# QKV projections as 64-row products in both row halves, with spread-out score maxima that add in PSUM

## The chip, the cores and the metric

The kernel runs on one core of a Trainium2 chip. The core has a matrix engine (TensorE, PE in the profile; its weight loads are listed apart as PEld), three engines for elementwise work (VectorE is DVE, ScalarE is ACT, GpSimd is POOL) and a queue that starts DMA transfers (SyncE, SP). Products land in PSUM, of which this kernel uses eight banks of 128 x 512 fp32. The metric is the time on the device in microseconds (us), the median over runs.

## The reference, cut to what matters

A transformer block on 2048 tokens of width 640, in fp32: layer norm, attention with 32 heads of 20, a residual, layer norm, a SwiGLU feed-forward of width 1728, a residual.

```python
B, S, D, H = 1, 2048, 640, 32            # F = 1728
def _A_ref(x, wqkv, wo):
    qkv = (x @ wqkv).reshape(B, S, 3, H, Dh).transpose(2, 0, 3, 1, 4)
    q, k, v = qkv[0], qkv[1], qkv[2]
    scores = einsum("bhqd,bhkd->bhqk", q, k) * (Dh ** -0.5)
    p = softmax(scores, axis=-1)
    o = einsum("bhqk,bhkd->bhqd", p, v)
    return o.transpose(0, 2, 1, 3).reshape(B, S, D) @ wo
h  = x + _A_ref(layernorm(x), wqkv, wo)
h2 = h + (silu(layernorm(h) @ w_gate) * (layernorm(h) @ w_up)) @ w_down
```

Here the projections `x @ wqkv` matter, and the row maxima of the scores that the softmax subtracts.

## The kernel before

**Precision.** fp32 operands are split into a high and a low part of a narrower type (`split`, L84): ScalarE rounds the high part, VectorE or GpSimd subtracts. A product is then three: high by high, low by high, high by low. With a depth of 640 = 5 x 128 rows, each output block takes 15 products that add up in one PSUM bank.

**Stages.** Layer norm, QKV projections and a part of the score maxima come first (to 367.6 us), then attention, the output projection and the feed-forward. The order of the instructions of every engine is the order in which the program issues them; no planner moves them. Only the first stage differs between the two kernels.

**The projection stage.** The tokens come in four chunks `c` of 512. A chunk has 18 slots (counted over the chunks in `slot[0]`): ten query or key blocks of 128 rows of the transposed result (`query_key`, 15 products of 128 rows and 512 columns, L447) and eight value halves (`value`, 15 products of 320 columns, L523), keys first. In the first chunk the first two blocks are made together by `first_blocks` (L471), and the slot after them is empty. When a block is done, `keep` copies it out of PSUM, splits it and stores it to memory (L486 to L513; the splits wait in `halved` for the next slot); for values, L531 copies. In the course of a chunk the next one is normalised (`norm`, L121, L122, L95 and L401 on VectorE, one or two steps behind each slot) and turned by transposes (`flip`, L417).

**The maxima.** The softmax of a later stage needs, for each query, the greatest score. A unit is a group of four heads (eight groups) and a query chunk. Two heads lie in rows 0 to 59 of a stacked tile and two in rows 64 to 123; so a product of 60 rows uses one row half of TensorE, and the `b` loop issues one for each half. `pair` picks the first or second head of a half, `t` the 128 queries, `kc` the key chunk. Some of the maxima are found during the projections, to fill VectorE's and ScalarE's time: all of unit 0 (`max_pair`, L171, one reduction over both 512-column results at L180), and key chunks 0 and 1 of several other units (`max_halves`, L182). For the latter the stored keys also hold, for half a chunk, the differences of two halves k1 - k2, so that the greater of two scores is q.k2 + relu(q.(k1 - k2)): a 512-column product gives q.k2 and q.(k1 - k2) side by side, ScalarE takes the positive part of the second into SBUF (L193), and VectorE adds and takes the maximum in one custom instruction for each row half (L195).

**What sets the order.** `urgent` (unit 0) and `early` (the rest) are lists of such jobs with a condition, mostly that the staged keys and queries were loaded at least two slots ago. `visit(n)` runs up to n of them; it is called once inside every block and value half and once after it, so that TensorE gets a cluster of two or three pairs of 60-row products. Staged keys and queries are loaded back from memory by `load_items` into five places, four of them shared with the raw weights (`raw`) and one apart (`fifth`); `stored_at` says from which slot on they are in memory.

**PSUM in this stage.** `ps_wide` has three places of two banks (maxima, and the first blocks), `ps_one` two places of one bank (projections and transposes).

Of the kernel before, what the change touches and what calls it, by code (L numbers as in the profile page):

```python
# [9 lines left out]
F32 = mybir.dt.float32  # L10
# [34 lines left out]
def tile_block(ctx: ExitStack, tc: tile.TileContext, x, wqkv, wo, wg, wu, wd, out):  # L45
# [125 lines left out]
    def max_pair(mx, q, k, pair, t, kc, k0):  # L171

        ps = ps_wide()
        for b in range(2):
            rows = slice(b * ROW, b * ROW + NPART)
            nc.tensor.matmul(
                ps[:, b, :], q[rows, pair, t * P : (t + 1) * P], k[rows, pair, k0 : k0 + CH],
                start=True, stop=True,
            )
        nc.vector.tensor_reduce(mx[:, :, pair, t, kc], ps, axis=AX.X, op=ALU.max)  # L180

    def max_halves(mx, q, k, pair, t, kc):  # L182


        ps = ps_wide()
        for b in range(2):
            rows = slice(b * ROW, b * ROW + NPART)
            nc.tensor.matmul(  # L188
                ps[:, b, :], q[rows, pair, t * P : (t + 1) * P], k[rows, pair, :],
                start=True, stop=True,  # L190
            )
        over = evp.tile([P, 2, CH // 2], F32, name="over", bufs=3)
        nc.scalar.activation(over, ps[:, :, CH // 2 :], AF.Relu)  # L193
        for b in range(2):
            nc.vector.tensor_tensor_reduce(  # L195
                over[:, b], ps[:, b, : CH // 2], over[:, b], 1.0, LOWEST, ALU.add, ALU.max,
                mx[:, b, pair, t, kc : kc + 1],
            )
# [22 lines left out]
    def max_finish(u):  # L221

        m = ps_one()[: G * TPC, :P]
# [46 lines left out]
    with tc.tile_pool(name="pa", bufs=2) as pa:  # L270
# [31 lines left out]
        fifth = pa.tile([P, 2, CH], F32R, name="fifth", bufs=1)  # L302

        def load_items():
            for n, (which, g, c, loaded, _) in enumerate(items):
                if loaded is not None:
                    continue
                if slot[0] < stored_at(which, g, c) or (n >= 5 and users[n - 5]):
                    return
                if n % 5 == 4:  # L310
                    t = fifth
# [7 lines left out]
        def staged_keys(g, c, kc, k, q):  # L319
            def one(t, pair):  # L320
                max_halves(mxs[g * NC + c], items[q][3], items[k][3], pair, t, kc)
                for n in (k, q):
                    users[n] -= 1
                load_items()
# [4 lines left out]
            pairs = [(t, pair) for t in moved(g * NC + c, kc) for pair in range(2)]  # L329
            for n in (k, q):  # L330
                users[n] += len(pairs)
            return [(ready, lambda a=a: one(*a)) for a in pairs]
# [25 lines left out]
        urgent = [a for kc in range(NC) for a in in_unit(0, kc, 18 * kc + 7)]  # L358
# [53 lines left out]
        def flip(c, k):  # L412
            if k == 0:
                zs[c] = z_tiles(c)
            ps = ps_one()
# [24 lines left out]

        def query_key(c, m):

            z_hi, z_lo = zs[c]
            ps = ps_wide()[:, 0, :] if slot[0] < 6 else ps_one()
            for n, (a, w) in enumerate(((z_hi, w_hi), (z_lo, w_hi), (z_hi, w_lo))):
                for k in range(ND):
                    nc.tensor.matmul(  # L447
                        ps, w[:, k, m * P : (m + 1) * P], a[:, k, :],
                        start=(n == 0 and k == 0), stop=(n == 2 and k == ND - 1),
                    )  # L450
                    if n == 1 and k == 3 and c:
                        visit(3)
            keep(c, m, ps)
# [1235 lines left out]
```

## Time and profile before

| | |
|---|---|
| median of 3 runs | 2083.9 us (2083.82 to 2086.28) |
| profiled execution, its own time | 2082.67 us |
| its span, first to last instruction | 2080.9 us |
| granted TensorE clock, mean | 1.000 |
| TensorE busy in the span | 2054.1 us |
| start to 22.24 us: first norm, transposes, first blocks | TensorE busy 14.41 us |
| 22.24 to 367.60 us: the rest of the projection stage | TensorE busy 338.05 us |
| 368 to 1400 us: attention | TensorE busy 1029.74 us |
| 1400 to the end: last of attention, output projection, feed-forward | TensorE busy 671.77 us |

A row of the profile's groups reads: line, engine, operation, output <- inputs, output shape <- input shape, count, then busy time and mean ns of one, then the idle time of the engine just before these instructions and what ended it. A row of the order of time reads: start, us, engine, line, operation, tile names, for a matmul rows*columns of the weights, shape, count, and in brackets the idle time before and what released the engine. Matmuls overlap each other in such rows: what one takes is told by the distance from one start to the next, not by the length.

### The profile page before, as it was taken

What the parts mean: (1) busy time and instruction counts of PE and PEld (TensorE: products, weight loads), DVE (VectorE), ACT (ScalarE), POOL (GpSimd) and SP (SyncE); (2) the same over time, 40 slices, a digit from 0 to 9 for tenths busy, and PEclk for the clock granted to TensorE, in tenths of its full rate; (3) what the DMA queues carried; (4) which work ended last, traced back from release to release, by engine and by line L of the source; (5) the groups of instructions that cost most, each with busy time, mean ns of one, the idle gap of its engine ahead of it and who ended that gap; (6) DMA issues with size and microseconds to landing.
All of it is one profiled execution on the core that took longest, in us unless ns stands there. A gap on an engine that the chain in (4) does not pass through costs nothing.

```text
span 2080.9 us, 37196 instructions
## 1 busy us (share of the span) xinstructions
PE 2054.1 (99%) x12636; PEld 1201.4 (58%) x12636; DVE 1659.7 (80%) x3631; ACT 1443.0 (69%) x2835; POOL 740.4 (36%) x1034
## 2 busy tenths in 40 slices
PE   8999999999999999999999999999999999999998
PEld 6666666433333343334333333335588888888888
DVE  7787867888888888888888888886368666676676
ACT  4657675999999999999999999996733222212221
POOL 2353331334343344343410001001145444753555
PEclk9999999999999999999999999999999999999999
DMA  8775544153444443534522213031139655884642
GB/s 263 222 220 169 164 143 127 49 167 103 145 138 131 138 134 115 170 125 160 172 97 63 47 37 104 22 116 60 35 123 308 238 191 165 322 286 159 200 150 92
DMA packets 192548, 305.37 MB, mean 147 GB/s; under 512 B 47440, under 2 KB 82256, under 8 KB 191336
## 3 DMA queue, kind: packets, MB, share of 16 engines
q1 hardware_dynamic: 186168, 280.18, 42.4%
q0 software_dynamic: 6096, 22.81, 3.5%
q8 instruction: 102, 1.67, 0.3%
q14 instruction: 86, 0.70, 0.1%
q10 hardware_dynamic: 96, 0.00, 0.0%
HBM read 203.82 MB, written 98.30 MB: 145 GB/s over the span
## 4 chain that ended last, share of the span: by engine, by line
PE 85%; DVE 5%; issue 3%; DMA 3%; POOL 2%; ACT 1%; SPq 1%; DVEq 0%; ACTq 0%; POOLq 0%
PE acc L991 23%; PE ps_a L1152 15%; PE ps_one L981 15%; PE ps_max L204 11%; PE ps_b L1246 8%; PE ps_one L523 3%; PE ps_wide L188 3%; PE ps_one L447 2%; DVE over L195 2%; PE ps_max L712 2%; DVE mx L180 1%; PE ps_b L712 1%; DMA halves<-j_d 1%; PE ps_wide L447 1%; POOL stage L800 1%
## 5 line engine op out<-in xcount | busy, mean ns | idle before, releaser
L987 ACT ACTIVATE probs<-ps_one 128x512 f32<-128x512 f32 x2048 | 1056.8, 616 | 61.7 <-PE ps_one L981 37.2
L210 DVE TENSOR_REDUCE mx<-ps_max 128x1 f32<-128x512 f32 x1472 | 925.7, 683 | 108.7 <-PE ps_one L981 79.1
L981 PE MATMUL ps_one<-q_stk,k_stk 62*128 62x512 f32 x2048 | 585.4, 450 | 2.6 <-DVE m L86 1.8
L991 PE MATMUL acc<-probs,v_stk 128*32 128x512 f32 x4096 | 545.1, 604 | 0.0
L981 PEld LDWEIGHTS ps_one<-q_stk,k_stk 62*128 62x128 f32 x2048 | 251.3, 184 | 431.8 <-ACT probs L987 397.5
L204 PE MATMUL ps_max<-k_stk,q_stk 60*128 60x512 f32 x1472 | 381.7, 425 | 0.0
L204 PEld LDWEIGHTS ps_max<-k_stk,q_stk 60*128 60x128 f32 x1472 | 271.7, 186 | 24.9 <-DVE mx L210 1.2
L195 DVE CUSTOM_DVE_ANT_0 over<-ps_wide,over 128x256 f32<-128x256 f32 x512 | 185.6, 420 | 68.1 <-ACT over L193 67.9
L1367 DVE TENSOR_TENSOR tmp<-ps_a,tmp 128x512 f32<-128x512 f32 x208 | 141.1, 689 | 120.6 <-PE ps_a L1152 93.5
L193 ACT ACTIVATE over<-ps_wide 128x512 f32<-128x512 f32 x256 | 139.2, 597 | 83.0 <-issue 39.9
L1026 POOL TENSOR_TENSOR o<-o,rb 128x512 f32<-128x512 f32 x31 | 39.9, 1287 | 411.9 <-DMA q_stk<-q_d 128.7
L1246 PE MATMUL ps_b<-halves,yp 128*128 128x320 f32 x1032 | 179.3, 308 | 1.9 <-DMA halves<-j_d 1.2
L991 PEld LDWEIGHTS acc<-probs,v_stk 128*32 128x32 f32 x4096 | 80.5, 108 | 173.7 <-issue 165.2
L1246 PEld LDWEIGHTS ps_b<-halves,yp 128*128 128x128 f32 x1032 | 165.1, 188 | 18.5 <-POOL yp L86 1.5
L1152 PE MATMUL ps_a<-t,units 128*128 128x512 f32 x624 | 162.6, 396 | 0.0
L1152 PE MATMUL ps_a<-z,units 128*128 128x512 f32 x516 | 133.9, 394 | 0.0
L86 POOL TENSOR_TENSOR yp<-y,yp 128x256 fp32r<-128x256 f32 x96 | 60.2, 627 | 188.3 <-ACT yp L85 188.3
L1152 PEld LDWEIGHTS ps_a<-t,units 128*128 128x128 f32 x624 | 112.5, 188 | 18.7
L1251 DVE TENSOR_TENSOR h<-ps_b,h 128x320 f32<-128x320 f32 x248 | 109.9, 480 | 6.9 <-PE ps_b L1246 5.4
L1152 PEld LDWEIGHTS ps_a<-z,units 128*128 128x128 f32 x516 | 93.1, 187 | 15.9
L85 ACT ACTIVATE yp<-tmp 128x512 fp32r<-128x512 f32 x40 | 25.3, 632 | 103.1 <-POOL tmp L1239 103.1
L1152 PE MATMUL ps_a<-z,lasts 128*128 128x512 f32 x324 | 92.5, 393 | 0.0
(209 smaller groups left out, 2253.4 us busy)
## 6 DMA issues: line engine op xcount, KB each, us to landing
units<-w_d SPq DMA_DIRECT2D x186, 256.0 KB
w_d<-stage SPq DMA_DIRECT2D x106, 256.0 KB
halves<-j_d SPq DMA_DIRECT2D x70, 320.0 KB
j_d<-stage SPq DMA_DIRECT2D x42, 320.0 KB
k_stk<-k_d SPq DMA_DIRECT2D x64, 160.0 KB
q_stk<-q_d SPq DMA_DIRECT2D x64, 160.0 KB
rb<-r_d SPq DMA_DIRECT2D x32, 256.0 KB
raw<-k_d SPq DMA_DIRECT2D x42, 160.0 KB
```

The lines of the kernel that those rows point to most:

```text
L193: nc.scalar.activation(over, ps[:, :, CH // 2 :], AF.Relu)
L195: nc.vector.tensor_tensor_reduce(over[:, b], ps[:, b, : CH // 2], over[:, b], 1.0, LOWEST, ALU.add, ALU.max, mx[:, b, pair, t, kc : kc + 1],)
L204: nc.tensor.matmul(ps, queries[u][rows, pair, t * P : (t + 1) * P], keys[u // NC][rows, pair, kc * CH : (kc + 1) * CH], start=True, stop=True,
L210: nc.vector.tensor_reduce(mxs[u][:, b, pair, t, kc : kc + 1], ps, axis=AX.X, op=ALU.max)
L447: nc.tensor.matmul(ps, w[:, k, m * P : (m + 1) * P], a[:, k, :], start=(n == 0 and k == 0), stop=(n == 2 and k == ND - 1),)
L981: nc.tensor.matmul(ps, keys[u // NC][rows, p, kt * P : (kt + 1) * P], queries[u][rows, p, :], start=True, stop=True,)
L987: nc.scalar.activation(probs[p][:, b, :], ps, AF.Exp, scale=scale)
L991: nc.tensor.matmul(acc[32 * j : 32 * j + 32, :], values[u // NC][:, kt, j * VW : j * VW + 32], probs[j // 2][:, j % 2, :], start=(kt == 0) ...
L1152: nc.tensor.matmul(ps.rearrange("p (t n) -> p t n", t=TPC), w[k][:, i], z[k][:, :, j], start=(first and m == 0), stop=(last and m == len(n ...
L1246: nc.tensor.matmul(ps, a, b, start=(n == 0), stop=(n == len(pairs) - 1))
L1251: nc.vector.tensor_tensor(out=h, in0=ps, in1=h, op=ALU.add)
L1367: add = lambda out, ps, x: nc.vector.tensor_tensor(out=out, in0=ps, in1=x, op=ALU.add)
```

## The change

A projection product of 128 rows is cut into two of 64 rows. `rounds` issues the upper one at once, and a lower one taken from `behind`, 21 jobs old; both halves of a block still add up in the same bank. Behind the last upper product of a block stands an empty VectorE instruction (`clobber_nop`) that names the bank. The copy-out (`keep`, `keep_value`) is issued with the last lower product; the splits (`split_later`) come seven 512-column products' worth of columns later.

PSUM is cut anew at the empty slot of the first chunk: three single banks `ps_one` for projections, five single banks `ps_max` for maxima and transposes. `max_pair` takes two of them with a reduction each. `max_four` replaces two calls of `max_halves` (both `pair`s of one `t`): four 256-column products make the differences, two to a bank; ScalarE takes their positive parts in place in PSUM; four more 256-column products add q.k2 to it; and VectorE reduces each bank once, giving two maxima. The two steps of `max_four` are separate: the second is put off by `BEHIND`.

`visit` no longer takes a number. It is called after every upper product and its partner and runs at most one job, paced by a count of columns issued: at least `BETWEEN` columns from job to job on the average and `SPACING` after the last one, and the second step of a job `BEHIND` columns after its first. Past slot 60 `urgent` comes first, before that `early`.

The rest follows from these: staged items have six places instead of five, loads of keys, queries and staged items are due one slot later, `urgent` starts one slot later, and at the end of the stage the remaining lower products are issued, with visits between them. The amount of products, maxima and transfers is the same.

```diff
     def max_pair(mx, q, k, pair, t, kc, k0):
-        ps = ps_wide()
-        for b in range(2):
+        banks = [ps_max() for _ in range(2)]
+        for b, ps in enumerate(banks):
             rows = slice(b * ROW, b * ROW + NPART)
             nc.tensor.matmul(
-                ps[:, b, :], q[rows, pair, t * P : (t + 1) * P], k[rows, pair, k0 : k0 + CH],
+                ps, q[rows, pair, t * P : (t + 1) * P], k[rows, pair, k0 : k0 + CH],
                 start=True, stop=True,
             )
-        nc.vector.tensor_reduce(mx[:, :, pair, t, kc], ps, axis=AX.X, op=ALU.max)
-    def max_halves(mx, q, k, pair, t, kc):
-        ps = ps_wide()
-        for b in range(2):
-            rows = slice(b * ROW, b * ROW + NPART)
-            nc.tensor.matmul(
-                ps[:, b, :], q[rows, pair, t * P : (t + 1) * P], k[rows, pair, :],
-                start=True, stop=True,
-            )
-        over = evp.tile([P, 2, CH // 2], F32, name="over", bufs=3)
-        nc.scalar.activation(over, ps[:, :, CH // 2 :], AF.Relu)
-        for b in range(2):
-            nc.vector.tensor_tensor_reduce(
-                over[:, b], ps[:, b, : CH // 2], over[:, b], 1.0, LOWEST, ALU.add, ALU.max,
-                mx[:, b, pair, t, kc : kc + 1],
-            )
+        for b, ps in enumerate(banks):
+            nc.vector.tensor_reduce(
+                mx[:, b, pair, t, kc : kc + 1], ps, axis=AX.X, op=ALU.max
+            )
+    def max_four(mx, q, k, t, kc):
+        banks = [ps_max() for _ in range(2)]
+        half = CH // 2
+        def products(cols, first):
+            for pair in range(2):
+                for b in range(2):
+                    rows = slice(b * ROW, b * ROW + NPART)
+                    nc.tensor.matmul(
+                        banks[b][:, pair * half : (pair + 1) * half],
+                        q[rows, pair, t * P : (t + 1) * P], k[rows, pair, cols],
+                        start=first and pair == 0, stop=True, skip_group_check=True,
+                    )
+        def differences():
+            products(slice(half, CH), True)
+            for ps in banks:
+                nc.scalar.activation(ps, ps, AF.Relu)
+        def maxima():
+            products(slice(0, half), False)
+            for b, ps in enumerate(banks):
+                nc.vector.tensor_reduce(
+                    mx[:, b, :, t, kc], ps.rearrange("p (j n) -> p j n", j=2),
+                    axis=AX.X, op=ALU.max,
+                )
+        return differences, maxima
...
-        m = ps_one()[: G * TPC, :P]
+        m = (ps_one if u else ps_max)()[: G * TPC, :P]
...
-                return 2 * block + 4
-            return 18 * c + 4 + block + (0 if which else ND)
+                return 2 * block + 4 + (block > 0)
+            return 18 * c + 5 + block + (0 if which else ND)
...
+        more = [pa.tile([P, 2, CH], F32R, name=f"raw{i}", bufs=1) for i in (5, 6)]
...
+            def four(t):
+                first, second = max_four(mxs[g * NC + c], items[q][3], items[k][3], t, kc)
+                def last():
+                    second()
+                    for n in (k, q):
+                        users[n] -= 1
+                    load_items()
+                first()
+                return last
...
+        urgent = [a for kc in range(NC) for a in in_unit(0, kc, 18 * kc + 8)]
...
-        def visit(n):
+        columns, due, seconds = [0], [0], []
+        BETWEEN, SPACING, BEHIND = 11 * CH // 2, 5 * CH, 13 * CH // 2
+        def visit():
             load_items()
-            for i in range(n):
-                for queue in (early, urgent) if i else (urgent, early):
-                    if queue and queue[0][0]():
-                        queue.pop(0)[1]()
-                        break
+            if seconds and columns[0] >= seconds[0][0]:
+                columns[0] += CH
+                seconds.pop(0)[1]()
+            if columns[0] < due[0]:
+                return
+            for queue in (early, urgent) if slot[0] < 60 else (urgent, early):
+                if queue and queue[0][0]():
+                    columns[0] += CH
+                    last = queue.pop(0)[1]()
+                    if last:
+                        seconds.append((columns[0] + BEHIND, last))
+                    due[0] = max(due[0] + BETWEEN, columns[0] + SPACING)
+                    return
+            due[0] = max(due[0], columns[0] - 4 * BETWEEN)
...
-            ps = ps_one()
+            ps = ps_max()
...
+        behind, splits = [], []
+        def second_half():
+            if behind:
+                f, done = behind.pop(0)
+                f(1)
+                if done:
+                    done()
+        def rounds(ps, n_columns, operands, done):
+            last = len(operands) - 1
+            for n, (a, b) in enumerate(operands):
+                def half(i, n=n, a=a, b=b):
+                    rows = slice(i * ROW, (i + 1) * ROW)
+                    nc.tensor.matmul(
+                        ps, a[rows], b[rows], start=(i == n == 0), stop=(i == 1 and n == last),
+                        skip_group_check=True,
+                    )
+                    if (i, n) == (0, last):
+                        nc.vector.clobber_nop([nc.vector.lower_ap(ps)])
+                half(0)
+                behind.append((half, done if n == last else None))
+                if len(behind) > 21:
+                    second_half()
+                columns[0] += n_columns
+                if slot[0] > 6:
+                    visit()
+                while splits and columns[0] >= splits[0][0]:
+                    splits.pop(0)[1]()
...
+            ps = ps_one()
+            cs = slice(m * P, (m + 1) * P)
+            rounds(
+                ps, CH,
+                [
+                    (w[:, k, cs], a[:, k, :])
+                    for a, w in ((z_hi, w_hi), (z_lo, w_hi), (z_hi, w_lo)) for k in range(ND)
+                ],
+                lambda: keep(c, m, ps),
+            )
...
+        def split_later(f):
+            splits.append((columns[0] + 7 * CH, f))
...
-            if slot[0] < 8:
+            if slot[0] < 10:
...
+                lambda: keep_value(c, t, half, ps),
+            )
+        def keep_value(c, t, half, ps):
+            finish_splits()
+            ev = evs[t % 2]
...
-                visit(2 if kind == "value" or slot[0] < 10 else 3)
-                finish_keep()
+                else:
+                    ps_ctx.close()
+                    ps_ctx = ExitStack()
+                    psum = ps_ctx.enter_context(
+                        tc.tile_pool(name="psum_p", bufs=1, space=bass.MemoryType.PSUM)
+                    )
+                    def ps_one():
+                        return psum.tile([P, CH], F32, name="ps_one", tag="ps_one", bufs=3)
+                    def ps_max():
+                        return psum.tile([P, CH], F32, name="ps_max", tag="ps_max", bufs=5)
...
+        while behind:
+            second_half()
+            columns[0] += CH
+            visit()
+        finish_splits()
```

More of the change, by code (lines that the diff above doesn't have):

```diff
@@ L307, in load_items @@
                     continue
-                if slot[0] < stored_at(which, g, c) or (n >= 5 and users[n - 5]):
+                if slot[0] < stored_at(which, g, c) or (n >= 6 and users[n - 6]):
                     return
-                if n % 5 == 4:
-                    t = fifth
+                if n % 6 >= 4:
+                    t = more[n % 6 - 4]
                 else:
@@ L319, in staged_keys @@
         def staged_keys(g, c, kc, k, q):
[L320 to L324, printed above, removed]
+            def four(t):
[7 more added lines that the diff above has]
+                return last
             def ready():
                 return all(items[n][3] is not None and slot[0] >= items[n][4] + 2 + (slot[0] < 24) for n in (k, q))
[L329 removed]
+            ts = moved(g * NC + c, kc)
             for n in (k, q):
[L331 to L332 removed]
+                users[n] += len(ts)
+            return [(ready, lambda t=t: four(t)) for t in ts]
         def unit_keys(u, kc, t, pair):
@@ L441, in query_key @@
         def query_key(c, m):
             z_hi, z_lo = zs[c]
[L444 to L449, printed above, removed]
-                    )
-                    if n == 1 and k == 3 and c:
-                        visit(3)
```

46 lines of the change are left out of this document (18 added, 28 removed).

## The prediction

> **What bounds the kernel now.** I read the page first, then the busy time of the stage that the diff touches, then TensorE's order of time inside that stage, and last the groups of that stage by shape.
>
> ```profile
> span 2080.9 us, 37196 instructions
> PE 2054.1 (99%) x12636; PEld 1201.4 (58%) x12636; DVE 1659.7 (80%) x3631; ACT 1443.0 (69%) x2835; POOL 740.4 (36%) x1034
> PE 85%; DVE 5%; issue 3%; DMA 3%; POOL 2%; ACT 1%; SPq 1%; DVEq 0%; ACTq 0%; POOLq 0%
> ```
>
> TensorE is busy for 99% of the span and carries 85% of the chain that ended last, so a microsecond less on it in one stage is a microsecond less in all, as long as the stages behind only start earlier. The diff touches the projection stage alone. From the first products of the third block (22.24) to the end of its last product it has this row (busy time by engine, instructions in brackets, granted clock):
>
> ```profile
> core 0: us, PE busy (x) PEld busy (x) DVE busy (x) ACT busy (x) POOL busy (x), PEclk, DMA share, GB/s
> 22.24:367.60 345.36, 338.05 (x1688) 230.06 (x1686) 267.39 (x1170) 217.23 (x406) 120.22 (x143) 1.00 0.59 181
> ```
>
> A busy TensorE is not one at its peak. Its order of time says what a product really takes, by the distance from one start to the next:
>
> ```profile
> 43.17 0.85 PE L176 MATMUL ps_wide<-k_stk,q_stk 60*128 60x512 f32 x4
> ...
> 66.38 0.66 PE L417 MATMUL ps_one<-ident,xt 128*128 128x128 f32 x4
> 66.79 0.97 PE L523 MATMUL ps_one<-w_hi,z_hi 128*128 128x320 f32 x5
> 67.60 0.75 PE L523 MATMUL ps_one<-w_lo,z_hi 128*128 128x320 f32 x4
> 68.28 0.74 PE L188 MATMUL ps_wide<-raw 60*128 60x512 f32 x4
> ...
> 103.86 1.33 PE L447 MATMUL ps_one<-z_hi,w_hi 128*128 128x512 f32 x5
> 105.03 1.09 PE L447 MATMUL ps_one<-z_lo,w_hi 128*128 128x512 f32 x4
> 106.05 0.97 PE L188 MATMUL ps_wide<-raw 60*128 60x512 f32 x6
> 106.95 0.50 PE L447 MATMUL ps_one<-z_lo,w_hi 128*128 128x512 f32 x1
> 107.29 1.33 PE L447 MATMUL ps_one<-z_hi,w_lo 128*128 128x512 f32 x5
> 108.55 0.81 PE L188 MATMUL ps_wide<-raw 60*128 60x512 f32 x4
> 109.55 0.49 PE L188 MATMUL ps_wide<-raw 60*128 60x512 f32 x2 [0.20 <-DVE mx L195]
> ...
> 363.53 0.51 PE L188 MATMUL ps_wide<-fifth,raw 60*128 60x512 f32 x2
> ```
>
> Five products of 128 rows and 512 columns take 103.86 to 105.03: 0.233 us each. Four from 105.03 to 106.05 take 1.02 where 0.93 was due: 0.09 for the change from 128-row to 60-row products. The three pairs of 60-row products (the two of a pair run in different row halves, at once) take 0.90 where 0.70 was due, and the first 128-row product after them 0.34 instead of 0.23. So one visit of 60-row products costs 0.09 + 0.20 + 0.10 = 0.39 us beyond its work. The 320-column products take (0.68 - 0.09) / 4 = 0.147.
>
> The nominal work of the stage, with counts from the code: 38 blocks of 15 products (570 x 0.233 = 132.8), 32 halves of values (480 x 0.147 = 70.6), 256 + 32 pairs for maxima (288 x 0.233 = 67.1), 15 flips of four transposes (0.41 each by 66.38 to 66.79, 6.2): 276.7 us of the 345.4. Of the 68.7 left, 121 stretches of 60-row products, the first at 43.17 and the last at 363.53, make 121 x 0.39 = 47.2. The remaining 21.5 are waits such as the 0.20 at 109.55.
>
> **The change, part by part.**
>
> *Row halves.* Each product of 128 rows becomes two of 64; the lower one runs 21 jobs later, next to the upper one of a later job, into another bank. The pairs at L188 show that two row halves run together at the pace of one (0.233 per pair at best), so a step of upper and lower is costed as one product. All max products then have the same tiling, and the 47.2 us go. New costs: the lag adds 21 steps (1050 jobs make 1071), and where a 320-column upper half stands beside a 512-column lower one or the reverse, the step takes the longer. From the built order: each of four sections of 120 value jobs has 99 steps of 320 columns, so 396 x 0.147 + 675 x 0.233 = 215.5 against 203.4 before: +12.1. The 15 flips and one transpose of the maxima stay 128-row products, but among 64-row ones: 16 x 0.39 = +6.2.
>
> *Maxima as four products of 256 columns.* The difference comes first, ScalarE takes its positive part in place, and the other products are added to it. 128 visits with four row pairs of 256 columns; from the rows below such a product takes (18.52 - 17.34) / 10 = 0.118, so 60.4 against 256 x 0.233 = 59.6: +0.8.
>
> ```profile
> 17.34 1.35 PE L471 MATMUL ps_one<-z_hi,w_hi 128*128 128x256 f32 x10
> 18.52 1.35 PE L471 MATMUL ps_one<-z_lo,w_hi 128*128 128x256 f32 x10
> ```
>
> TensorE's own work thus falls by 47.2 - 12.1 - 6.2 - 0.8 = 28.1 us.
>
> *Waits.* This decides. The groups of the stage, and three places that show how a bank is handed on:
>
> ```profile
> L195 DVE CUSTOM_DVE_ANT_0 over<-ps_wide,over 128x256 f32<-128x256 f32 x512 | 185.6, 420 | 68.1 <-ACT over L193 67.9
> L193 ACT ACTIVATE over<-ps_wide 128x512 f32<-128x512 f32 x256 | 139.2, 597 | 83.0 <-issue 39.9 <-PE ps_wide L188 39.1 <-DVE mx L195 1.9
> L210 DVE TENSOR_REDUCE mx<-ps_max 128x1 f32<-128x512 f32 x72 | 45.2, 683 | 8.3 <-PE ps_one L981 4.1 <-PE ps_max L204 3.9
> L531 ACT ACTIVATE ev<-ps_one 128x320 f32<-128x320 f32 x32 | 14.0, 438 | 8.4 <-PE ps_one L523 8.4
> L121 DVE BATCH_NORM_STATS2 st<-xt 128x6 f32<-128x320 f32 x32 | 14.0, 479 | 3.5 <-DMA xt<-in_A_x 3.5
> L494 ACT ACTIVATE e<-ps_one 128x512 f32<-128x512 f32 x20 | 12.0, 598 | 15.7 <-issue 8.6 <-PE ps_one L447 7.1
> L401 DVE TENSOR_SCALAR xt<-xt,mv,r_a 128x640 f32<-128x640 f32 x16 | 11.1, 724 | 0.1
> ```
> ```profile
> 387.81 0.39 PE L204 MATMUL ps_max<-k_stk,q_stk 60*128 60x512 f32 x1
> 388.24 1.89 DVE L210 TENSOR_REDUCE mx<-ps_max 128x1 f32<-128x512 f32 x3 [0.23 <-PE ps_one L981]
> ```
> ```profile
> 109.15 1.08 ACT L193 ACTIVATE over<-ps_wide 128x512 f32<-128x512 f32 x2
> 109.32 0.08 DVE L195 DVE_READ_ACCUMULATOR2_ANT mx<- 128x1 f32 x1
> 109.52 0.22 PEld L188 LDWEIGHTS ps_wide<-raw 60*128 60x128 f32 x2 [0.47 <-ACT v_stk L494]
> ```
> ```profile
> 147.30 1.21 DVE L180 TENSOR_REDUCE mx<-ps_wide 128x2 f32<-128x1024 f32 x1
> 148.57 0.50 PE L188 MATMUL ps_wide<-raw 60*128 60x512 f32 x2 [0.94 <-DVE mx L180]
> ```
>
> VectorE itself is no bound: 320 reductions of 512 elements, (1.89 - 0.68) / 2 = 0.605 apart, are 194 us where 212 went before (512 x 0.345 + 32 x 1.13, both from distances of starts), in some 275 us. But a visit holds two of five banks from its first product to its reduction, and the second bank of visit k+2 is the first of visit k. Visits stand at least 6 steps apart (1.4 us). From the last product into that bank to its reuse the order has 0.82 us of TensorE work at 73 places, about 1.0 at 23. Needed are 0.28 for the product (0.39 for 512 columns at 387.81, less 256 columns), 0.04 until VectorE starts (388.20 to 388.24), 0.68 for the reduction, and 0.06 (148.51 to 148.57) or 0.15 (109.40 to 109.55) until TensorE goes on: 1.06 to 1.15. A product that had to wait loses another 0.10, as its weights come late. So the wait costs 0.34 to 0.43 at 73 places and 0.16 to 0.25 at 23: up to 37 us. Against it, a wait lets the upper row half run ahead by one product of 0.12 or even 0.23, which widens the 0.82 by as much: down to nothing. I take 0.25 and 0.07, nearer to the 148.57 row since it shows a plain reduction: 18.3 + 1.6 = 20.
>
> *Other waits.* Statistics and application of the norm stand in VectorE's queue between reductions, in bursts of 2 x 0.48 + 0.21 = 1.17 or two times 0.72; a visit of 1.7 us with 1.2 of reductions leaves 0.5. Some 13 bursts fall among dense visits: 13 x 0.6 = 8 us (0 where nothing waits, 13 x 1.2 = 16 at most). Around slot 8, visits of 1.2 every 1.4 us meet copies and norm steps on VectorE: 5 us (0 to 8). The second products wait for two positive parts, 0.48 + 0.60 after the first ones, and have 1.76 us for it, 1.6 needed: 3 us for copies in between (0 to 33, below). The empty VectorE instruction at the end of each tile makes the first lower product, six jobs on (1.4 us), wait for VectorE's queue; I cost it at nothing, because a visit's two reductions (1.2) fit into that, and count its share in the 5 and 8.
>
> *What moves at no cost.* Copies are due 21 jobs later and splits seven columns' worth after them, on POOL (120 of 345 us busy); loads of staged items are due a slot later, with six places instead of five; SP and POOL issue the same transfers. Cover gone, each would be a wait of TensorE for a load, which the waits of before show with 0.3 us in the whole stage.
>
> *Sum.* Before's waits go (21.5), TensorE's work falls by 28.1, new waits come to 20 + 8 + 5 + 3 = 36: -13.6 us. The profiled execution took 2082.67 with a span of 2080.9; the median of the three runs is 2083.9, 1.2 above it. Taken off the median: 2070 us.
>
> **The rivals.**
>
> *No wait at all:* the row halves drift apart and the banks come in time. For it: only 0.24 us are missing at most places. Against it: the norm's bursts remain. -49.6 + 8 gives 2042.
>
> *The positive part comes late (slower).* Place: second products, queued behind a ScalarE that also does 32 copies, 32 splits and 30 copies of values, 0.44 to 0.60 each, in this stage. One in front of a pair pushes it by up to 0.5 with 0.16 to spare: 0.35 x 94 = 33 us at worst, in place of my 3: 2100. It decides from 0.19 per such operation. That it writes PSUM is shown nowhere in this trace; L193 into SBUF is the nearest row. For it: ScalarE is the releaser in most of VectorE's idle time (67.9 us at L195).
>
> *Issue.* A step is now four instructions on TensorE. The densest long run in the trace is L471 with 0.118 for one load and one product; at twice that a 320-column step takes 0.236: 396 x 0.089 + 675 x 0.003 = 37 us, 2107. Against it: after the wait at 109.52 two loads and two products start within 0.04 us. [...]
>
> *It doesn't do what it says:* row halves of one accumulation run one after the other, +215 us; the pairs at L188 speak against it.
>
> **How the numbers follow.** Forecast 0.52 (its own range 2055 to 2088), no wait 0.12, late positive part 0.25, issue 0.08, no overlap 0.03. Runs of this kernel differ by 2.5 us, so 0.2% (4.2 us) is what can be told from no change. Faster: 0.40 of the forecast and all of the second, 0.52. Same: 0.09 and 0.05, 0.14. Slower: 0.03, 0.20, 0.08, 0.03, 0.34. The range leaves out half of the no-wait case, and issue and no overlap: 2050 to 2104.
>
> **What would show it.** Right: 64-row products in steps of 0.233 and 0.147, no 0.39 around maxima, the stage ending near 354 instead of 367.6, and waits of TensorE for the reductions of about 20 us. Wrong: steps of 0.236 for 320 columns, waits of the second products for the positive part above 15 us, or a stage with neither wait that ends before 335.

## The result, and the profile after

The changed kernel takes 2087.7 us (median of 17 runs, 2084.5 to 2091.4) beside 2083.4 for the kernel before on the same chips: a ratio of 1.0021, 95% interval 1.0014 to 1.0029. The forecast was 2070. It is slower by 4.3 us where 13.6 less was expected, so some 18 us have to be found. All runs behind the ratios had a mean granted clock of 0.99 or more; one of the four runs of e5_even, at 0.851, took 2196.8 us and is left out of its median and ratio.

The page after (profiled execution 2087.61, span 2085.5), its lines on the span, the engines and the shares of the chain by engine:

```profile
span 2085.5 us, 39669 instructions
PE 2049.9 (98%) x14198; PEld 1251.5 (60%) x14198; DVE 1642.5 (79%) x2895; ACT 1440.5 (69%) x2835; POOL 744.3 (36%) x1039
PE 91%; DMA 4%; DVE 2%; issue 1%; ACT 1%; SPq 1%; POOL 0%; DVEq 0%; ACTq 0%; POOLq 0%
```

The page's answer on cores gives the first clue: the mean granted clock of TensorE, 1.000 before, is now

```profile
core 0: 2085.5 us, clock 0.995
```

Half a per cent of 2085.5 us is 10.4 us. Stretches of the span show where (columns: the stretch, its length, busy time of PE, PEld, DVE, ACT and POOL, granted clock, share of DMA, GB/s):

```profile
26.00:36.00 10.00, 10.00 (x32) 7.70 (x31) 4.48 (x10) 1.90 (x4) 0.00 (x0) 0.50 0.67 229
36.00:38.00 2.00, 2.00 (x19) 1.62 (x18) 0.40 (x1) 0.00 (x0) 0.00 (x0) 0.93 0.00 0
132.00:146.00 14.00, 9.38 (x63) 7.95 (x63) 1.67 (x7) 4.81 (x9) 7.87 (x10) 0.76 0.88 266
373.00:379.00 6.00, 5.97 (x29) 2.60 (x29) 3.98 (x7) 4.98 (x11) 5.38 (x3) 0.72 0.70 198
```

What a stretch loses is estimated as its length times one minus its clock (at the clock of 0.50, five products of 512 columns take 2.13 us, from 31.74 to 33.87; at full clock they start 0.23 to 0.24 us apart, from 344.88 to 345.35): 10 x 0.50 + 2 x 0.07 = 5.1, 14 x 0.24 = 3.4, 6 x 0.28 = 1.7, together 10.2. Ahead of each of the three drops stands an idle TensorE, in its order of time (the bracket holds the idle time and what ended it). The second drop comes at 138.7 us; the 0.78 us of idle at 132.14 were followed by none:

```profile
25.56 0.84 PE L491 MATMUL ps_one<-z_hi,w_hi 64*128 64x512 f32 x2 [2.55 <-DVE z_lo L86]
```
```profile
132.14 0.49 PE L491 MATMUL ps_one<-z_hi,w_hi 64*128 64x512 f32 x1 [0.78 <-ACT e L564]
```
```profile
138.68 0.55 PE L194 MATMUL ps_max<-raw 60*128 60x256 f32 x1 [2.55 <-DMA raw<-q_d]
```
```profile
141.16 0.77 PE L194 MATMUL ps_max<-raw 60*128 60x256 f32 x3 [1.93 <-DMA raw<-q_d]
```
```profile
372.82 0.57 PE L1066 MATMUL ps_one<-q_stk,k_stk 62*128 62x512 f32 x2 [0.74 <-ACT e L564]
```

The last idle stretch is not new. The kernel before has it too, and its clock stayed at 1.00 there:

```profile
368.46 0.57 PE L981 MATMUL ps_one<-q_stk,k_stk 62*128 62x512 f32 x2 [0.73 <-ACT e L494]
```

The first four are new, 2.55 and 5.26 us. The 10.2 us of clock do not all come on top of them. From 139.23 to 141.16 the clock was halved while TensorE stood idle anyway, which takes about 1.0 off. And the 1.7 behind the last stretch hardly shows: from the first product of attention to the end of the span pass 1712.7 us (2085.5 - 372.8), as against 1712.4 before (2080.9 - 368.5). That leaves 2.55 + 5.26 + 5.1 + 2.4 + 0.2 = 15.5 us of the 17.9 that the forecast missed by (4.3 + 13.6). Everything else the prediction priced must then have come out right as a sum to some 2 us; that does not show that each term did. The next lines look at them. First the row halves, after a flip and before a visit:

```profile
85.38 0.30 PE L491 MATMUL ps_one<-w_hi,z_hi 64*128 64x320 f32 x1
85.38 0.31 PE L491 MATMUL ps_one<-w_hi,z_lo 64*128 64x320 f32 x1
85.52 0.30 PE L491 MATMUL ps_one<-w_hi,z_hi 64*128 64x320 f32 x1
85.53 0.31 PE L491 MATMUL ps_one<-w_hi,z_lo 64*128 64x320 f32 x1
```

An upper and a lower half start together and the next pair 0.14 to 0.15 us later: here two halves cost one product (0.147 us in the prediction), and four instructions (two weight loads and two products) fit into it. Then the waits of the stage (engine, tile and line, what it waited for: us in total, times, longest):

```profile
DVE mx L208 <- PE ps_max L194: 51.7, 100, 1.8
PEld ps_max L194 <- DVE mx L208: 31.2, 75, 1.5
```

Weight loads of visits stand still 75 times for a reduction. In a dense stretch VectorE shows the loop of the banks:

```profile
184.53 1.29 DVE L208 TENSOR_REDUCE mx<-ps_max 128x2 f32<-128x512 f32 x2 [0.35 <-PE ps_max L194]
186.17 1.29 DVE L208 TENSOR_REDUCE mx<-ps_max 128x2 f32<-128x512 f32 x2 [0.35 <-PE ps_max L194]
187.80 1.29 DVE L208 TENSOR_REDUCE mx<-ps_max 128x2 f32<-128x512 f32 x2 [0.34 <-PE ps_max L194]
```

A visit takes 1.64 us where the order asks for 1.4: reduction waits for products, products wait for the bank that the reduction holds. That is the 0.25 us per visit of the prediction; VectorE itself is idle for 0.35 us of each round, so it is not the bound.

### The profile page after: what moved, and what is told of

Its sections match the earlier page's. It is cut to its first block, busy times and chain, and to the rows that moved or that the text cites. A ratio compares the mean times of both kernels' runs of the same rounds, so it can differ in the third digit from the quotient of the medians.

```text
span 2085.5 us, 39669 instructions
## 1 busy us (share of the span) xinstructions
PE 2049.9 (98%) x14198; PEld 1251.5 (60%) x14198; DVE 1642.5 (79%) x2895; ACT 1440.5 (69%) x2835; POOL 744.3 (36%) x1039
## 4 chain that ended last, share of the span: by engine, by line
PE 91%; DMA 4%; DVE 2%; issue 1%; ACT 1%; SPq 1%; POOL 0%; DVEq 0%; ACTq 0%; POOLq 0%
PE acc L1076 24%; PE ps_one L1066 16%; PE ps_a L1237 14%; PE ps_max L219 12%; PE ps_one L491 9%; PE ps_b L1331 7%; PE ps_max L194 4%; PE ps_max L797 2%; PE ps_b L797 1%; DVE mx L208 1%; DMA halves<-j_d 1%; DMA raw<-q_d 1%; DMA t<-t_d 1%; PE ps_max L451 0%; PE ps_max L176 0%
## 5 line engine op out<-in xcount | busy, mean ns | idle before, releaser
L208 DVE TENSOR_REDUCE mx<-ps_max 128x2 f32<-128x512 f32 x256 | 164.7, 686 | 67.9 <-PE ps_max L194 51.7
L203 ACT ACTIVATE ps_max<-ps_max 128x512 f32<-128x512 f32 x256 | 137.2, 579 | 55.5 <-PE ps_max L194 52.1
L86 POOL TENSOR_TENSOR yp<-y,yp 128x256 fp32r<-128x256 f32 x96 | 60.2, 627 | 188.0 <-ACT yp L85 188.0
L491 PE MATMUL ps_one<-z_hi,w_hi 64*128 64x512 f32 x380 | 117.7, 407 | 3.8 <-DVE z_lo L86 2.5
L491 PE MATMUL ps_one<-z_lo,w_hi 64*128 64x512 f32 x380 | 117.7, 404 | 0.0
L491 PE MATMUL ps_one<-z_hi,w_lo 64*128 64x512 f32 x380 | 115.4, 400 | 0.0
```

The lines of the kernel that those rows point to most:

```text
L203: nc.scalar.activation(ps, ps, AF.Relu)
L208: nc.vector.tensor_reduce(mx[:, b, :, t, kc], ps.rearrange("p (j n) -> p j n", j=2), axis=AX.X, op=ALU.max,)
L491: nc.tensor.matmul(ps, a[rows], b[rows], start=(i == n == 0), stop=(i == 1 and n == last), skip_group_check=True,)
```

## The experiments

Ratios are to the kernel before, run on the same chip in turn. 0.001 is 2.1 us.

**The re-cut of PSUM.** The idle stretch at 25.56 ends with VectorE's part of the split of the first blocks (`keep`, L86), the last instruction that reads their banks: TensorE's first product in the new layout waited for it, with 2.55 us of idle time. The chain there:

```profile
23.02 0.34 DVE z_hi L557
...
23.39 0.90 ACT z_hi L85 x2
24.29 0.50 ACT z_lo L85
...
24.81 0.70 DVE z_lo L86
...
25.56 0.49 PE ps_one L491
```

The first experiment keeps the three projection banks from the start.

```diff
-        return psum.tile([P, 2, CH], F32, name="ps_wide", tag="ps_wide", bufs=3)
+        return wide.tile([P, 2, CH], F32, name="ps_wide", tag="ps_wide", bufs=2)
...
-        return psum.tile([P, CH], F32, name="ps_one", tag="ps_one", bufs=2)
+        return psum.tile([P, CH], F32, name="ps_one", tag="ps_one", bufs=3)
...
-                    ps_ctx.close()
-                    ps_ctx = ExitStack()
+                    wide_ctx.close()
```

> The changed kernel with another layout of PSUM: the three banks of the projections stay from the first transposes on, and only the wide banks of the transposes (two places instead of three) give way to the five of the maxima at the empty slot; no product there has to wait for the copies of the first blocks. Theory A (TensorE's idle stretch of 2.55 us at 25.56 halves the clock that is granted from 26 to 36 us): the stretch goes (-2.6) and the clock there is 1.00, which gives back half of the 10.3 us at half clock (-5.2); the third transpose pays up to 0.5 for one place less. Sum -7.3 us: 2080. Theory B (the clock falls because for 21 products only the upper row half works, whatever stood ahead of it): the stretch goes but the clock stays at 0.50 for some 10 us: -2.1 us, 2085.5.

Measured: 2082.6, ratio 0.9990 (0.9981 to 1.0000), 0.0031 or 6.5 us below the changed kernel. In its profile the stretch is gone and the clock is full, then the second trouble is worse than before:

```profile
22.00:38.00 16.00, 15.80 (x112) 12.57 (x113) 12.95 (x26) 8.16 (x15) 1.47 (x2) 1.00 0.84 268
130.00:144.00 14.00, 7.85 (x57) 7.14 (x59) 2.58 (x4) 4.58 (x9) 3.12 (x5) 0.63 0.75 235
```

Upper halves alone, with no idle time ahead of them, kept the full clock here (1.00 from 22 to 38 us): theory B falls. Of the gain some 2 us went back at the second trouble, where TensorE now comes earlier to loads that do not come as much earlier: its three idle stretches there (0.76, 3.67 and 2.87 us, ending at 129.08, 133.25 and 136.67) are 7.3 us as against 5.3. The half clock is longer too (10.4 us by the 0.63 over 14 us, as against 6.8), but about half of it falls on an idle TensorE.

**Which rows work.** e6 leaves the waits and gives the lonely halves a partner.

```diff
                 if len(behind) > 21:
                     second_half()
+                else:
+                    beside(a[ROW:], b[ROW:])
...
         while behind:
             second_half()
+            beside(w_hi[:ROW, 0, :P], z[:ROW, 0, :])
```

> The changed kernel with products beside those that run alone: while the first 21 upper halves are issued, each has a lower half of the same operands beside it, which goes to a bank that nobody reads; and the last 21 lower halves have an upper half beside them. The waits stay. Theory A (the clock comes back late, 10.3 us after the idle stretch at 25.56 instead of about 3.6 as in e3_rows128, because half of the rows are idle; and the 0.74 us of idle at 372.82 cost a stretch of half clock only for the same reason): 6.7 us less at half clock at the start (-3.4) and about 3 us less at the end (-1.5): 2083. Theory B (the rows in use do not matter): within 1 us of 2087.7, and half clock from 26 to 36 us as before.

Measured: 2084.9, ratio 0.9999 (0.9990 to 1.0008), 4.6 us below the changed kernel. The clock at the start, after the same 2.55 us of idle, which end at 24.93 here:

```profile
24.00:26.00 2.00, 1.07 (x6) 0.88 (x8) 1.90 (x4) 2.00 (x5) 0.54 (x1) 0.72 0.96 324
26.00:28.00 2.00, 2.00 (x12) 1.59 (x10) 1.97 (x5) 1.39 (x3) 0.00 (x0) 0.50 1.05 389
28.00:30.00 2.00, 2.00 (x18) 1.60 (x16) 0.10 (x1) 0.00 (x0) 0.00 (x0) 0.93 1.03 337
```

(1 - clock) x length is 0.56 + 1.00 + 0.14 = 1.7 us lost, as against 5.1: half clock followed the 2.55 us of idle in both runs, for 3.4 us with all rows in use and for 10.2 with half of them. The second half of the expectation failed: at the end of the stage the clock fell all the same, and for longer (0.50 to 0.57 from 373 to 380 us, in a profiled execution of 2086.93 us). What decides there stays open.

The 10.2 us are no fixed price. Between 20 and 400 us the clock of the changed kernel was 0.50 for 10.24, 6.83 and 3.41 us (from 26.04, 138.68 and 374.20 on); by the windows of the other runs it was so for up to 13.6 us in e2 (0.66 from 20 to 40 us) and up to 34.2 in e3 (its rows from 155 to 195 us, below), and all five are whole multiples of 3.41 within the rounding. In the changed kernel the first lower half starts at 33.0 and the clock is back at 36.3 us; in e2 and e4, with this stall and lone upper halves behind it, it is back at 38.3 and 36.9 (0.67 and 0.81 from 35 to 40 us). Whether the clock waited for the lower halves was not shown: no run moved their start on purpose.

**The burst of transfers.** From 118.8 us up to the product at 138.68 the changed kernel has no visits. The chain in that time holds a run of projection products, then SyncE's issues and a load:

```profile
118.81 8.86 PE ps_one L491 x74
...
127.86 1.39 SPq L148
...
134.02 7.05 DMA raw<-q_d
141.07 0.09 issue
141.16 0.77 PE ps_max L194 x3
```

Two explanations offered themselves: the visits behind it start too early, or there were none for too long. e2 tried the first.

```diff
-                return all(items[n][3] is not None and slot[0] >= items[n][4] + 2 + (slot[0] < 24) for n in (k, q))
+                return all(items[n][3] is not None and slot[0] >= items[n][4] + 2 + (slot[0] < 30) for n in (k, q))
```

> The changed kernel, but up to slot 30 (before: up to slot 24) a maximum may only use staged keys and queries that were asked for three slots ago instead of two. Theory A (visits at 136 to 141 us stand in TensorE's queue for loads that are still in a burst of transfers, and the clock is halved behind that): the 4.5 us of idle at 138.68 and 141.16 go, and the 6.5 us at half clock with them (3.3): -7.8 us, 2080; a part of it is paid again where the visits are made up later (0 to 2 us). Theory B (the visits only wait later instead, because the burst moves with them, or the postponed visits crowd others): within 2 us of 2087.7.

Measured: 2085.3, ratio 1.0003 (0.9994 to 1.0013), 3.8 us less: half of theory A. The wait moved: TensorE now stood idle for 2.55 us up to 144.07, before a projection product. ScalarE's copy out of an earlier block had ended at 144.02, after 5.73 us of waiting for the store that still read its buffer:

```profile
143.42 0.60 ACT L564 ACTIVATE v_stk<-ps_one 128x512 f32<-128x512 f32 x1 [5.73 <-DMA k_d<-v_stk]
```

So the transfers are the cause, not the visits alone. e5, on the layout of e1, stretches the first maxima so that they last.

```diff
-                    due[0] = max(due[0] + BETWEEN, columns[0] + SPACING)
+                    due[0] = max(due[0] + (16 * CH // 2 if slot[0] < 24 else BETWEEN), columns[0] + SPACING)
```

> The kernel of e1_no_switch with the visits of the first 24 slots at least 8 columns' worth (of 512) apart on the average instead of 5.5, so that the maxima of the first chunk last until those of the second can be loaded: in the order of the program slots 22 to 25 get 5, 5, 4 and 0.5 half visits instead of none. Theory A (the first maxima run out, the blocks of slots 22 to 25 follow each other in 3.5 us, their stores and loads crowd into one burst of transfers, and TensorE waits for it and loses its clock): the idle stretches of e1 at 129.08, 133.25 and 136.67 (7.3 us) go and the half clock in 120 to 160 us (0.87 x 40: 5.2 us) with them: -8 to -12 us against e1, 2071 to 2075. Theory B (the transfers of the second chunk are late whatever the visits do): within 3 us of e1's 2082.6.

Measured: 2071.3, ratio 0.9932 (0.9913 to 0.9952), 0.0058 or 12 us below e1 and 14 us below the kernel before (10 to 18 by the interval). The stretch in question:

```profile
118.00:146.00 28.00, 26.77 (x238) 22.14 (x240) 22.91 (x45) 14.44 (x26) 15.88 (x20) 0.94 0.81 261
```

The changed kernel's answer for the same 28 us is

```profile
118.00:146.00 28.00, 22.74 (x178) 18.91 (x178) 7.91 (x25) 9.65 (x15) 19.49 (x23) 0.88 0.79 233
```

60 products more in the same time, with DMA as busy as in the changed kernel: with visits among them, the blocks of slots 22 to 25 no longer follow each other in 3.5 us, and no product waits for a load. The loads of staged keys that were late (`raw<-k_d` on SyncE) are issued from 112.0 us on, as against 127.5 in the changed kernel; in the kernel before the first of them went out at 111.0. Theory A holds. What is left of the half clock, the 0.94 (3.4 us), stands behind another stall: 1.76 us of idle up to 118.55, where a product waits for a reduction that stands behind the norm's steps on VectorE (1.84 us on L97 in the chain). Of the versions that do all the work, none that was run is clearly faster than this one (three runs).

**The mode changes.** e3 puts the 128-row products back and leaves the spread maxima.

```diff
-                half(0)
-                behind.append((half, done if n == last else None))
-                if len(behind) > 21:
-                    second_half()
+                nc.tensor.matmul(ps, a, b, start=(n == 0), stop=(n == last))
+                if n == last:
+                    done()
```

> The changed kernel with the row halves undone: each projection product is one of 128 rows again, with no lag, and everything else (spread visits, positive parts in PSUM, banks) as changed. Theory A (each change between 128-row and 60-row products costs 0.39 us in all, as in the prediction): 288 stretches of 60-row products x 0.39 = 112 us, less what these pauses hide of the waits for reductions (up to 20) and less the lag and the flips' changes (4.9 + 4.9 + 6.2): between 2087.7 + 76 = 2164 and 2184. Theory B (spread changes cost little, the 0.39 was a matter of the clusters of before): below 2110.

Measured: 2162.8 (two runs), ratio 1.0373 (1.0352 to 1.0394), 73 us above the changed kernel: theory B falls, though A's window begins at 2164. What a change costs can be read from e3's rows:

```profile
361.04 0.53 PE L194 MATMUL ps_max<-raw 60*128 60x256 f32 x4
361.50 0.49 PE L489 MATMUL ps_one<-z_hi,w_lo 128*128 128x512 f32 x1
361.92 0.50 PE L194 MATMUL ps_max<-raw 60*128 60x256 f32 x4
```

From one visit to the next, with one projection product between them, 0.88 us pass where the work asks for 0.24 + 0.23: 0.41 us too many, close to the 0.39 of the prediction. The total is less clean, as part of it is clock again: 41 us at half clock as against 20 in the changed kernel, some 10 of the 73 us. Without them the sum lies below A's window, and what hid the rest was not taken apart. The clock is lost here in a form not seen elsewhere. The answer for three stretches of e3:

```profile
155.00:160.00 5.00, 3.27 (x11) 2.10 (x11) 1.29 (x2) 3.08 (x6) 2.73 (x4) 0.60 0.69 212
160.00:190.00 30.00, 30.00 (x101) 18.30 (x99) 14.03 (x24) 9.04 (x17) 6.02 (x8) 0.50 0.45 134
190.00:195.00 5.00, 5.00 (x34) 4.23 (x33) 2.58 (x4) 2.51 (x5) 1.05 (x1) 0.98 0.13 42
```

For 30 us TensorE is never idle by its records and still gets half the clock (15 us lost), while it goes to and fro between 128-row and 60-row products. The stretch begins with 2.56 us of idle (up to 156.73). The same to and fro runs at full clock from 190.2 us to the end of the stage, so the changes alone did not take the clock; why it stayed at 0.50 for so long is open.

**The bank and the reduction.**

```diff
-                    mx[:, b, :, t, kc], ps.rearrange("p (j n) -> p j n", j=2),
+                    mx[:, b, :, t, kc], ps.rearrange("p (j n) -> p j n", j=2)[:, :, : half // 2],
```

> The changed kernel with each of the 256 reductions of the spread maxima reading half of its columns (128 of each 256), so that half of these maxima are left out; nothing else differs. A reduction of 256 elements should take some 0.4 us instead of 0.69. Theory A (the bank of a visit is handed on too late by its reduction, some 20 us in the stage as predicted, and the norm's steps between reductions cost another 8): -15 to -25 us, 2063 to 2073. Theory B (the row halves drift apart and hide it): within 3 us of 2087.7.

Measured: 2066.4, ratio 0.9911 (0.9895 to 0.9928), 0.0110 or 23 us below the changed kernel: theory A. The groups of the two weight loads of these maxima, first in the changed kernel and then in e4 (after the bar busy time and mean ns, then the idle time before and its releasers):

```profile
L194 PEld LDWEIGHTS ps_max<-raw 60*128 60x128 f32 x512 | 59.8, 189 | 21.8 <-DVE mx L208 14.1 <-issue 5.0 <-ACT ps_max L203 0.3
L194 PEld LDWEIGHTS ps_max<-raw,raw 60*128 60x128 f32 x512 | 59.0, 186 | 19.5 <-DVE mx L208 17.1
```

```profile
L194 PEld LDWEIGHTS ps_max<-raw 60*128 60x128 f32 x512 | 58.6, 189 | 10.6 <-issue 2.9 <-ACT ps_max L203 1.0 <-ACT ev L600 0.9
L194 PEld LDWEIGHTS ps_max<-raw,raw 60*128 60x128 f32 x512 | 58.3, 186 | 8.9 <-DVE xt L435 2.1 <-DVE mx L208 1.9 <-ACT ps_max L203 0.5
```

Of 31.2 us behind reductions these rows still name 1.9; the stage's waits of e4 have 2.7 us at 9 places. Two smaller edits on e5 tried to split that price. First the steps of the norm:

```diff
+                if n == 6 and slot[0] % 18 >= 5 and lns:
+                    lns.pop(0)()
...
-                for _ in range(2 if j >= 5 else 1):
-                    if j >= 1 and lns:
-                        lns.pop(0)()
+                if j >= 1 and lns:
+                    lns.pop(0)()
```

> The kernel of e5_even with the steps of the norm set apart: where two steps stood in a row behind each slot (from the sixth slot of a chunk on), one now comes in the middle of the slot's products and one behind them. Theory A (a burst of two norm steps on VectorE, up to 1.4 us, holds up the reductions and through them the banks: the prediction's 8 us): -3 to -8 us against e5's 2071.3, 2063 to 2068. Theory B (the bursts are hidden, the waits are those of the bank alone): within 2 us of e5.

Measured: 2072.9, ratio 0.9937 (0.9922 to 0.9951): no difference to e5 that can be told, as theory B has it. It is not proof that the bursts cost nothing: e7's trace has a stall of its own, 2.60 us up to 84.77 behind ScalarE's copy of values with 3.4 us at half clock, in which a gain of some 4 us can hide, and e5's 1.76 us at 118.55 are such a burst. Then the time for which a bank is held:

```diff
-        BETWEEN, SPACING, BEHIND = 11 * CH // 2, 5 * CH, 13 * CH // 2
+        BETWEEN, SPACING, BEHIND = 11 * CH // 2, 5 * CH, 6 * CH
```

> The kernel of e5_even with the second step of each spread maximum 6 columns' worth of 512 behind the first instead of 6.5, so that each bank is held some 0.12 us less. Theory A (the bank's reuse is what binds, and the positive part has room: 1.64 us for 1.6 needed): up to 0.12 x 96 = 11 us less, I expect -3 to -8 against e5, 2063 to 2068. Theory B (the positive part binds: what the banks gain, the second products wait): 0 to +6, 2071 to 2077.

Measured: 2071.1, ratio 0.9941 (0.9925 to 0.9958): again no difference to e5 that can be told (some 5 us either way by the intervals). Theory A's 3 to 8 us less did not come. The waits of weight loads for reductions are 26.2 us at 65 places as against 27.4 at 68 in e5; those for the positive part rose from 1.0 to 1.6. So e4 shows what long reductions cost; that it is the time for which a bank is held, as the prediction has it, rests on the loop in the rows at 184.53 and is not shown by e8. Last the lag:

```diff
-                if len(behind) > 21:
+                if len(behind) > 17:
```

> The kernel of e5_even with the lower half 17 jobs behind instead of 21. Theory A (the lag costs its steps at both ends and late copies, and the wait behind the empty VectorE instruction is covered): 4 steps less with the upper half alone and 4 with the lower alone, 8 x 0.233 x 1/2 = 0.9, and copies and stores 1 us earlier: -1 to -3 us against e5. Theory B (the cover is gone: between the last upper product of a block and its first lower one there are now 2 jobs, 0.5 us, instead of 6, while VectorE may be inside a reduction of 0.69 with another behind it): 70 blocks and value halves x 0.2 to 0.4 = +14 to +28, 2085 to 2099.

Measured: 2075.4, ratio 0.9956 (0.9943 to 0.9969), 5 us above e5: neither. The wait behind the empty VectorE instruction, 1.8 us where the groups name it, is far from theory B; but one visit met

```profile
86.45 1.28 PE L196 MATMUL ps_max<-raw,raw 60*128 60x256 f32 x4 [5.08 <-ACT ps_max L205]
```

ScalarE had waited, with that positive part behind it in its queue, until a store of values gave a buffer back (6.32 us of transfer in the chain), and the clock was 0.50 from 85 to 90 us. That stall is as long as the whole difference to e5: this one late transfer decided more than the four steps of lag.

## Why the prediction was wrong

Its range held the time; its sign was wrong. Step by step:

- *What moves at no cost* failed. It said that copies and splits 21 jobs later and loads one slot later cost nothing, since waits for loads stood in the kernel before "with 0.3 us in the whole stage". Measured: 0.78 + 2.55 + 1.93 = 5.3 us of waits, and some 2.4 us more through half clock while TensorE worked. The late stores alone did not do it: the visits were spread so thick in the first chunk that they ran out before the second chunk's keys could be loaded, so that four slots ran at 3.5 us each while their transfers needed more (e2, e5). I counted instructions and their columns, but not, slot by slot, whether a visit was ready.
- A step was missing: the re-cut of PSUM at the empty slot. Nothing in the prediction says who must be done before the first new bank is given out. It cost 2.55 us of idle and 5.1 of half clock; in e1, where both are gone, 6.5 us came back.
- The clock was taken as 1.00 throughout because before's row said so. By the rows half clock took 10.2 us in three places, of which some 7.7 show in the time: the dearest single term. Idle times of 2.55 us at 25.56 and 138.68, and of 0.74 at 372.82, were followed by half clock; behind the first of them it lasted 3.4 us where all rows work (e6) and 10.2 where half do.
- *Row halves*: the pace was right (0.15 us a pair at 85.38), and so was the price of the changes that they save (0.41 in e3). The gain of 28.1 as a whole was not measured by itself. The lag's +12.1 was too much, by up to 7 us by estimate (the 21 added steps of 0.233 make 4.9 of it): it charged steps of 320 beside 512 columns as the longer. Here they drift, with 320 columns at 344.91, 345.06, 345.21 beside 512 at 344.88, 345.12, 345.35:

```profile
344.88 0.39 PE L491 MATMUL ps_one<-z_hi,w_hi 64*128 64x512 f32 x1
344.91 0.31 PE L491 MATMUL ps_one<-w_lo,z_hi 64*128 64x320 f32 x1
345.06 0.31 PE L491 MATMUL ps_one<-w_hi,z_lo 64*128 64x320 f32 x1
345.12 0.39 PE L491 MATMUL ps_one<-z_hi,w_hi 64*128 64x512 f32 x1
345.21 0.31 PE L491 MATMUL ps_one<-w_hi,z_lo 64*128 64x320 f32 x1
345.35 0.39 PE L491 MATMUL ps_one<-z_hi,w_hi 64*128 64x512 f32 x1
```

- *Waits* for the bank: 20 us were forecast, mostly at 73 places. In the trace weight loads wait for reductions for 31.2 us at 75 places, in part while the other row half goes on, and e4 gives 23 us back for shorter reductions. The 8 us for the norm's bursts within the total are neither borne out nor excluded by e7; the total of 36 was not taken apart further. Nor was the 21.5 us of waits that were to go with the kernel before: it is the remainder of a sum, where TensorE's own idle time in that stretch was 7.3 us (345.36 - 338.05).
- *Rivals*: "no wait at all" falls with e4, "issue" with the steps of 0.15 us at 85.38, "no overlap" with the pairs there. "The positive part comes late" named the right sign but the wrong place: weight loads waited 0.3 us for it in the whole stage.

With the two stalls taken out (e5), the kernel takes 0.9932 of the time before, 14 us less, as against the 13.6 that were forecast. Part of that is the thinner visits themselves, so the agreement is no proof of every term.

## What to carry to other kernels

When a change makes products denser, ask of each slot what is left to fill it while transfers catch up: this stage ran out of it at 118.8 us and waited 5.3 us behind that, and with filler left there it took 12 us less (e5 beside e1). Price an idle stretch of TensorE at its length plus the half clock that the trace shows behind it: here 2.55 us of idle cost 5.1 more by estimate where half of the rows worked afterwards, and 1.7 where all did (e6). The new layout of PSUM in mid-stage cost those 2.55 us, which were gone in e1: let what is needed first keep its banks.

## What the runs showed of the hardware

- 2.55 us of idle were followed by half clock for 10.2 us with 64 of 128 rows in use, for 3.4 us with all of them (e6); without idle time ahead, 64 rows alone kept a clock of 1.00 from 22 to 38 us (e1).
- From 20 to 400 us the clock was 0.50 for 10.24, 6.83 and 3.41 us in the changed kernel, for up to 13.6 in e2 and up to 34.2 in e3: each a whole multiple of 3.41 us.
- 0.73 us of idle before attention left the clock at 1.00 in the kernel before, 0.74 us in the changed one were followed by 0.72 over 6 us; partners for the last lower halves did not help (e6: 0.50 to 0.57 from 373 to 380 us), and in e1 and e2 the same 0.74 us were followed by a clock of 1.00 up to 420 us.
- TensorE without a gap, but changing between 128-row and 60-row products, stayed at a clock of 0.50 from 160 to 190 us, behind an idle stretch of 2.56 us; from 195 us on the same changes ran at 1.00 (e3).
- Products in the two row halves did not go in pairs at 344.88 to 345.35 us of the changed kernel: those with 320 columns started 0.15 us apart beside those with 512 columns, 0.23 to 0.24 apart. The first lower half starts at 33.02 us, ahead of the upper one that the program issues before it (34.30).
